# A fused attention and MoE kernel: one scale of s per chunk of tiles, the low parts of x on VectorE in every pair, the small products first in a tile, and the first loads on two queues

## The chip, the cores and the metric

The kernel runs on one core of a Trainium2 chip. The metric is the device time of one execution in microseconds (us): 1389.33 us, the median of 3 runs (1389.17 to 1389.57). Everything is float32 at the kernel's boundary except the two weight matrices, which come as float64.

## The reference

The input x has 8 batches of 4160 rows of 192 columns, which makes 33,280 tokens. A causal window of 7 taps is softmaxed for each of 8 heads and weighs the last 7 rows of x. The result goes through one MoE block with 1024 hidden columns.

```python
def _attn_ref(x, weight_gen):
    w = softmax(weight_gen, axis=-1)            # 8 heads, 7 taps
    ...
    out = np.einsum('bshk,bskhg->bshg', w, x_unf)
def _moe_ref(x, w_in, w_out, g_ln):
    h = x @ w_in
    h_max = np.max(h, axis=-1, keepdims=True)
    e = np.exp(h - h_max)
    sm = e / (np.sum(e, axis=-1, keepdims=True) + 1e-09)
    solu = h * sm
    mu = np.mean(solu, axis=-1, keepdims=True)
    var = np.mean((solu - mu) ** 2, axis=-1, keepdims=True)
    ln = (solu - mu) / np.sqrt(var + 1e-06) * g_ln
    return (ln @ w_out).astype(np.float32)
```

`w_in` and `w_out` arrive as the two 32-bit words of each double, and the kernel puts float32 numbers together from them on the chip.

## The kernel before, in words

**Tiling.** Each of the 128 partitions holds 260 consecutive tokens (`RUN`), so a batch of 4160 tokens lies on 16 partitions (`PB`), and a tile is one token of every partition: 128 rows. There are 260 tiles. The rows come in 18 chunks: one of 4 tiles, two of 8 and fifteen of 16. The attention works in groups of 4 tiles (the first group in two of 2), 66 groups in all, and TensorE turns the rows over two tiles at a time (a pair, 130 in all).

**The tokens before a run.** The window of a partition's first tokens reaches 6 tokens back (`HALO`), into the last tokens of the partition before it. L78 loads them for 127 partitions at once, with 1152 numbers each, into partitions 1 to 127. Where a batch begins the window holds zeros: L75 clears partition 0, and L80 copies a tile of zeros over the 8 partitions at which a batch begins. L79 loads the first four tiles themselves.

**A group of tiles.** The taps' softmax of a chunk is seven steps, t0 to t6: VectorE's maximum (L112), GpSimd's subtraction (L114), ScalarE's exponential (L118), VectorE's sum (L120), ScalarE's copy (L122), VectorE's reciprocal (L124) and GpSimd's product (L126). GpSimd then multiplies the seven shifted windows of x with the taps (L133), adds the products in two steps (L139, L141) and leaves two halves, `half`, which has two buffers. VectorE adds them into `a` (L366, the step `fin`, three buffers of four tiles) and ScalarE copies 64 of its columns once more (L372, `dup`).

**A pair.** TensorE transposes two tiles into `pa` (L383, `xT`), and ScalarE rounds them to a high part `x_hi` (L391, `xhi`). In every second pair TensorE then subtracts the high part in place (L398, `xn`) and ScalarE rounds the rest to `x_lo` (L405, `xlo`). In the pairs between, VectorE subtracts and rounds in one instruction (L412, `xld`). `VECTOR_PAIRS = 2` sets that.

**A tile.** The first product (`mm1`) fills one of three PSUM tiles `h` of 1024 columns: for each half of the columns three matmuls over 128 rows of x (L422), and then six over the 64 rows that are left, two of them on the two halves of the array's rows at a time (L427). VectorE takes the negated maximum of `h` (L441, `max`), bounds its size by the larger of it and 0.5 (L445, `vb`) and takes the reciprocal (L450, `vr`): that is the scale of s of that row. ScalarE makes the exponentials and their sum (L454, `exp`). VectorE multiplies h, scale and exponentials into s, over `h` itself, and sums it (L460, `solu`). ScalarE sums the squares (L466, `sq`) and rounds s to float16 (L473, `hi`). VectorE makes the float16 rest (L477, `lo`). SyncE's queue transposes both by DMA (L485, `tr`), and TensorE multiplies them with the prepared `w_out` in 24 matmuls (L529, `mm2`). ScalarE scales the result into `ot` (L540, `out`), and every four tiles are stored (L543, `od`). `mm1` of a tile waits until `sq` and `lo` of the tile three before it are done with `h`. The eight small steps f0 to f7 of a group of rows (`scales`: L497 on VectorE, L500 to L516 on ScalarE) make the last factor from the sums.

**The order.** Every engine runs its own list in order, and `issue_order` writes these lists: it walks through a model of the engines with a cost in ns for each step, and among the steps that are ready on an engine takes the one whose tile number plus the number in the table `URGENCY` is the smallest. Loads go to SyncE's queue in the order of the same walk; the weights' loads and the first two chunks' are issued ahead of it.

## Time and profile before

| | |
|---|---|
| median of 3 runs | 1389.33 us |
| the profiled execution | 1389.4 us |
| its span | 1387.5 us, so 1.9 us lie around it |
| TensorE clock granted | 0.991 |
| busy: TensorE matmul, VectorE, ScalarE, GpSimd | 1259.2, 1230.0, 1128.5, 1247.0 us |
| moved by DMA | 210.43 MB |

In a profile PE is TensorE, PEld its weight loads, DVE is VectorE, ACT ScalarE, POOL GpSimd and SP the SyncE queue. A row of the timeline gives the start, the duration, the engine, the line of the kernel and the operation, and in brackets how long the engine had been idle before it and what ended that. A row of the groups by line gives the busy time in all and the mean in ns. A row of the windows gives, for a stretch from one time to another, each engine's busy time and instructions. Busy shares of four engines between 81% and 91% of a span don't say by themselves which of them sets the end.

### The profile page before, as it was taken

How to read it: one execution, taken by the hardware profiler on the slowest of the kernel's cores; microseconds unless marked ns; L12 is line 12 of the kernel's file. 1: busy time of each engine (PE TensorE's matmuls, PEld its weight loads, DVE VectorE, ACT ScalarE, POOL GpSimd, SP SyncE). 2: the span in 40 equal slices, each digit the busy share in tenths (PEclk: the TensorE clock that was granted, in tenths of full speed). 3: DMA queues.
4: the chain of work that ended last, by engine and by line, in shares of the span. 5: the costliest groups of instructions: out<-in, count | busy, mean ns of one | idle time of the engine just before them, and what ended most of it. 6: DMA issues, size and time to landing. Idle time of an engine off the chain costs nothing.

```text
span 1387.5 us, 26562 instructions
## 1 busy us (share of the span) xinstructions
PE 1259.2 (91%) x10028; PEld 988.6 (71%) x10028; DVE 1230.0 (89%) x2068; ACT 1128.5 (81%) x2231; POOL 1247.0 (90%) x243
## 2 busy tenths in 40 slices
PE   0389899999999999989989999999999999999997
PEld 0267677777777777767767677777777777777776
DVE  2999898999989899889989898989899889999984
ACT  1588887888888888888888888888788888888885
POOL 1999999999999999999999999999999999999100
PEclk9989999999999999999999999999999999999999
DMA  3469768696968789697857768687858668766765
GB/s 90 139 142 194 147 128 201 124 207 122 194 130 174 146 145 195 122 198 123 186 130 166 158 149 186 118 190 145 193 109 191 146 140 176 132 133 117 134 131 116
DMA packets 565241, 210.43 MB, mean 152 GB/s; under 512 B 544329, under 2 KB 545785, under 8 KB 565112
## 3 DMA queue, kind: packets, MB, share of 16 engines
q1 hardware_dynamic: 565112, 208.73, 72.5%
q8 instruction: 79, 1.29, 0.4%
q14 instruction: 50, 0.41, 0.1%
HBM read 46.19 MB, written 25.56 MB: 52 GB/s over the span
## 4 chain that ended last, share of the span: by engine, by line
POOL 51%; DVE 16%; issue 13%; ACT 13%; PE 4%; DMA 3%; SPq 0%; POOLq 0%; DVEq 0%; ACTq 0%
POOL pr L133 27%; POOL pr L139 15%; POOL half L141 6%; DVE h L460 5%; ACT hl L473 4%; DVE hl L477 4%; ACT e L466 3%; DVE stats L441 3%; ACT e L454 3%; DVE a L366 3%; DMA xt<-in_x_dram 2%; POOL wt L114 2%; PE po L529 2%; POOL wt L126 1%; PE h L422 1%
## 5 line engine op out<-in xcount | busy, mean ns | idle before, releaser
L133 POOL TENSOR_TENSOR pr<-xt,wt 128x5376 f32<-128x5376 f32 (+1 forms) x66 | 631.3, 9565 | 23.1 <-DMA xt<-zeros 20.5
L529 PE MATMUL po<-w_hl,hlT 128*128 128x192 f16 x6192 | 558.5, 247 | 26.6 <-ACT ot L540 26.2
L529 PEld LDWEIGHTS <-hlT 128*128 128x128 f16 x6240 | 515.2, 98 | 82.2 <-issue 79.2
L477 DVE SCALAR_TENSOR_TENSOR hl<-h,hl 128x1024 f16<-128x1024 f32 x260 | 315.4, 1220 | 44.2 <-ACT e L466 31.5
L460 DVE SCALAR_TENSOR_TENSOR h<-h,stats,e 128x1024 f32<-128x1024 f32 x260 | 334.7, 1288 | 22.4 <-ACT e L454 9.2
L473 ACT ACTIVATE hl<-h 128x1024 f16<-128x1024 f32 x260 | 267.3, 1028 | 92.3 <-DVE stats L497 57.4
L139 POOL TENSOR_TENSOR pr<-pr 128x2304 f32<-128x2304 f32 (+1 forms) x66 | 332.7, 5041 | 5.2
L441 DVE TENSOR_REDUCE stats<-h 128x1 f32<-128x1024 f32 x260 | 316.1, 1216 | 8.9 <-PE h L427 8.1
L454 ACT ACTIVATE e<-h,stats 128x1024 f32<-128x1024 f32 x260 | 292.6, 1126 | 31.1 <-DVE stats L441 27.2
L466 ACT ACTIVATE e<-h,stats 128x1024 f32<-128x1024 f32 x260 | 292.3, 1125 | 5.9 <-DVE hl L477 5.4
L422 PE MATMUL h<-wa_hi,x_hi 128*128 128x512 f32 x520 | 225.4, 433 | 36.3 <-ACT e L466 22.8
L141 POOL TENSOR_TENSOR half<-pr 128x1536 f32<-128x1536 f32 (+1 forms) x66 | 225.8, 3422 | 5.2
L422 PE MATMUL h<-wa_hi,x_lo 128*128 128x512 f32 x520 | 207.5, 399 | 0.8 <-ACT x_lo L405 0.8
L422 PE MATMUL h<-wa_lo,x_hi 128*128 128x512 f32 x520 | 206.3, 397 | 0.0
L422 PEld LDWEIGHTS h<-wa_hi,x_hi 128*128 128x128 f32 x520 | 98.9, 190 | 59.3 <-ACT e L466 26.0
L427 PE MATMUL h<-wb_hi,x_hi 64*128 64x512 f32 x520 | 131.1, 500 | 0.0
L383 PE MATMUL pa<-ident,a 128*128 128x128 f32 x520 | 84.6, 286 | 44.2 <-DVE a L366 44.1
L540 ACT ACTIVATE ot<-po,stats 128x192 f32<-128x192 f32 x258 | 111.4, 432 | 8.5 <-PE po L529 8.5
L366 DVE TENSOR_REDUCE a<-half 128x768 f32<-128x1536 f32 (+1 forms) x66 | 116.4, 1764 | 1.6 <-POOL half L141 1.6
L427 PEld LDWEIGHTS h<-wb_hi,x_hi 64*128 64x128 f32 x520 | 48.6, 184 | 96.7 <-issue 96.7
L422 PEld LDWEIGHTS h<-wa_hi,x_lo 128*128 128x128 f32 x520 | 98.6, 190 | 24.3 <-ACT x_lo L405 1.6
L383 PEld LDWEIGHTS pa<-ident,a 128*128 128x128 f32 x520 | 55.8, 142 | 79.7 <-DVE a L366 44.1
(79 smaller groups left out, 1194.1 us busy)
## 6 DMA issues: line engine op xcount, KB each, us to landing
out_dram<-ot SPq DMA_DIRECT2D x65, 384.0 KB, 3.3
xt<-in_x_dram SPq DMA_DIRECT2D x30, 576.0 KB, 4.7
xt<-in_x_dram SPq DMA_DIRECT2D x30, 480.0 KB, 4.7
wt<-in_weight_gen_dram SPq DMA_DIRECT2D x15, 448.0 KB, 4.1
hlT<-hl SPq DMA_TRANSPOSE x260, 4.5
raw<-in_moe_w_out_dram SPq DMA_DIRECT2D x1, 1536.0 KB, 9.4
xt<-in_x_dram SPq DMA_DIRECT2D x3, 384.0 KB, 6.0
raw_a<-in_moe_w_in_dram SPq DMA_DIRECT2D x2, 512.0 KB, 11.5
```

The source lines that it names most:

```text
L133: nc.gpsimd.tensor_tensor(out=window(pr, 0, [(TG * D, K), (HG, n * H), (1, HG)]), in0=window(xt, t * D, [(D, K), (HG, n * H), (1, HG)]), i ...
L139: nc.gpsimd.tensor_tensor(out=pr[:, :3], in0=pr[:, :3], in1=pr[:, 3:6], op=ALU.add)
L141: nc.gpsimd.tensor_tensor(out=half, in0=window(pr, 0, [(2 * TG * D, 2), (D, n), (1, D)]), in1=window(pr, TG * D, [(5 * TG * D, 2), (D, n), ...
L422: nc.tensor.matmul(h[:, fs], lhs[:, 0, :], rhs[:, fs], start=n == 0, stop=False)
L427: nc.tensor.matmul(h[:, fs], lhs[rows, 1, :], rhs[rows], start=False, stop=n == 2,)
L441: nc.vector.tensor_reduce(stat(t, NMAX), h_of[t], axis=AX.X, op=ALU.max, negate=True)
L454: nc.scalar.activation(e, h_of[t], AF.Exp, bias=stat(t, NMAX), accum_out=stat(t, Z))
L460: nc.vector.scalar_tensor_tensor(out=h, in0=h, scalar=stat(t, SIGMA), in1=e, op0=ALU.mult, op1=ALU.mult, accum_out=stat(t, M))
L466: nc.scalar.activation(e_of.pop(t), h_of[t], AF.Square, bias=stat(t, M), scale=-float(FF), accum_out=stat(t, Q),)
L473: nc.scalar.activation(hl[:, 0, :], h_of[t], AF.Copy, scale=2.0**14)
L477: nc.vector.scalar_tensor_tensor(out=hl[:, 1, :], in0=h_of[t], scalar=2.0**14, in1=hl[:, 0, :], op0=ALU.mult, op1=ALU.subtract,)
L529: nc.tensor.matmul(po[:, :D], hlT[:, half * NJ + j, :], w2_hl[:, j, w, :], start=n == 0, stop=n == len(terms) - 1,)
```

## The change

Four things are changed, and the order of the work is made anew with them.

1. **The first loads.** L75 now clears the 6 tokens ahead on all 128 partitions, the loads of the tokens before a run are eight, one per batch, of 15 partitions each, and no zeros are copied. Half of the eight go to ScalarE's queue, and so do the first 128 rows of `w_in`, half of `w_out` and `g_ln`.
2. **The scale of s.** It is one number per partition and chunk, 1/(0.5 + norm), where the norm is the root of the sum of x's squares over this chunk and the one before it, times a factor from the largest sizes in `w_in`. The steps v00 to v03 square x on ScalarE, a quarter of a chunk at a time (L145, 768 numbers a partition), and v1 to v5 are seven instructions on one number a partition. n0 to n6 make the factor from `w_in` once. `vb` and `vr` are gone, and of f0 to f7 one activation and one reduction of a group are gone as well.
3. **x's low parts.** `VECTOR_PAIRS = 1`: every pair goes the way of L412, which is L479 now; `xn` and `xlo` no longer run.
4. **The order of a tile's matmuls.** The six over 64 rows (L491 now) come first in `mm1`, then the six over 128 rows (L494).

The table `URGENCY` and the model's costs are new (GpSimd's product and first sum of a group count 14990 ns instead of 14206, for example), and w_in's first 128 rows are converted ahead of its last 64.

```diff
-            nc.gpsimd.memset(xt[:1, : HALO * D], 0.0)
-            zeros = const.tile([B, D], F32, name="zeros")
-            nc.gpsimd.memset(zeros, 0.0)
-            nc.sync.dma_start(xv[1:, :HALO, :], x_run[: P - 1, RUN - HALO :, :])
+            nc.gpsimd.memset(xt[:, : HALO * D], 0.0)
             nc.sync.dma_start(xv[:, HALO : HALO + n, :], x_run[:, :n, :])
-            nc.sync.dma_start(
-                xv[::PB, :HALO, :], zeros.unsqueeze(1).broadcast_to([B, HALO, D])
-            )
+            for b in range(B):
+                queue = nc.sync if b % 2 else nc.scalar
+                queue.dma_start(
+                    xv[b * PB + 1 : (b + 1) * PB, :HALO, :],
+                    x_run[b * PB : (b + 1) * PB - 1, RUN - HALO :, :],
+                )
...
+            nc.scalar.activation(
+                junk[:, : (r1 - r0) * D].rearrange("p (t d) -> p t d", d=D), xv[:, r0:r1, :],
+                AF.Square, accum_out=squares_x[:, c + 1, part : part + 1],
+            )
...
     for f in range(2):
+        nc.scalar.dma_start(raw_a[:, f * FF : (f + 1) * FF], w_in[:P, f * FF : (f + 1) * FF])
         nc.sync.dma_start(raw_b[f * D2 : (f + 1) * D2, :], w_in[P:, f * FF : (f + 1) * FF])
...
-        for fs in halves:
-            for n, (lhs, rhs) in enumerate(((hi, wa_hi), (hi, wa_lo), (lo, wa_hi))):
-                nc.tensor.matmul(h[:, fs], lhs[:, 0, :], rhs[:, fs], start=n == 0, stop=False)
         for n, (lhs, rhs) in enumerate(((hi, wb_hi), (hi, wb_lo), (lo, wb_hi))):
             for f, fs in enumerate(halves):
                 rows = slice(f * D2, (f + 1) * D2)
-                nc.tensor.matmul(
-                    h[:, fs], lhs[rows, 1, :], rhs[rows], start=False, stop=n == 2,
-                )
+                nc.tensor.matmul(h[:, fs], lhs[rows, 1, :], rhs[rows], start=n == 0, stop=False)
+        for fs in halves:
+            for n, (lhs, rhs) in enumerate(((hi, wa_hi), (hi, wa_lo), (lo, wa_hi))):
+                nc.tensor.matmul(h[:, fs], lhs[:, 0, :], rhs[:, fs], start=False, stop=n == 2)
...
-            out=h, in0=h, scalar=stat(t, SIGMA), in1=e, op0=ALU.mult, op1=ALU.mult, accum_out=stat(t, M)
+            out=h, in0=h, scalar=row(t, SCALE), in1=e, op0=ALU.mult, op1=ALU.mult, accum_out=stat(t, M)
...
-VECTOR_PAIRS = 2
+VECTOR_PAIRS = 1
```

SyncE's queue at the start of the program, before: the taps of chunk 0 (`wt`), the last rows of `w_in` (`hl`), the tokens ahead of the runs (127 partitions), the first four tiles of x, and the first rows of `w_in` (`raw_a`) with the copy of zeros between their two halves.

```order
1 L96 DMA wt<-in_weight_gen_dram 128x224
2 L152 DMA hl<-in_moe_w_in_dram 64x1024 x2
3 L78 DMA xt<-in_x_dram 127x1152
4 L79 DMA xt<-in_x_dram 128x768
5 L168 DMA raw_a<-in_moe_w_in_dram 128x1024
6 L80 DMA xt<-zeros 8x6x192
7 L168 DMA raw_a<-in_moe_w_in_dram 128x1024
```

The same queue in the changed kernel, where `raw_101` is half of `w_out`:

```order
1 L96 DMA wt<-in_weight_gen_dram 128x224
2 L76 DMA xt<-in_x_dram 128x768
3 L79 DMA xt<-in_x_dram 15x1152 x4
4 L196 DMA hl<-in_moe_w_in_dram 64x1024 x2
5 L96 DMA wt<-in_weight_gen_dram 128x448
6 L202 DMA raw_101<-in_moe_w_out_dram 128x4x384
7 L85 DMA xt<-in_x_dram 128x1536
```

And ScalarE's list there, which issues its own loads ahead of its first arithmetic:

```order
1 L56 ACT_TABLE_LOAD
2 L79 DMA xt<-in_x_dram 15x1152 x4
3 L195 DMA raw_a<-in_moe_w_in_dram 128x1024 x2
4 L202 DMA raw_101<-in_moe_w_out_dram 128x4x384
5 L206 DMA g<-in_moe_g_ln_dram 128x8x1
6 L118 ACTIVATE wt<-wt 128x224
7 L145 ACTIVATE junk,squares_x<-xt 128x1920
8 L122 ACTIVATE wy<-wm 128x32
```

The 127 partitions have become eight times 15 on two queues, and the last rows of `w_in` have moved behind x.

TensorE near the program's start, before, where a pair's high part is subtracted (`minus`) and a tile's first product follows:

```order
93 L398 MATMUL pa<-x_hi,minus 128x256 x2
94 L422 MATMUL h<-wa_hi,x_hi 128x512
95 L422 MATMUL h<-wa_lo,x_hi 128x512
96 L422 MATMUL h<-wa_hi,x_lo 128x512
97 L422 MATMUL h<-wa_hi,x_hi 128x512
98 L422 MATMUL h<-wa_lo,x_hi 128x512
99 L422 MATMUL h<-wa_hi,x_lo 128x512
100 L427 MATMUL h<-wb_hi,x_hi 128x512 x2
101 L427 MATMUL h<-wb_lo,x_hi 128x512 x2
102 L427 MATMUL h<-wb_hi,x_lo 128x512 x2
```

And in the changed kernel:

```order
86 L491 MATMUL h<-wb_hi,x_hi 128x512 x2
87 L491 MATMUL h<-wb_lo,x_hi 128x512 x2
88 L491 MATMUL h<-wb_hi,x_lo 128x512 x2
89 L494 MATMUL h<-wa_hi,x_hi 128x512
90 L494 MATMUL h<-wa_lo,x_hi 128x512
91 L494 MATMUL h<-wa_hi,x_lo 128x512
92 L494 MATMUL h<-wa_hi,x_hi 128x512
93 L494 MATMUL h<-wa_lo,x_hi 128x512
94 L494 MATMUL h<-wa_hi,x_lo 128x512
```

The two subtractions of a pair are gone, and the paired small matmuls stand ahead.

VectorE in the middle of the program, before, up to a group's sum (`a`), with the two small instructions between a tile's maximum and its s:

```order
716 L445 TENSOR_REDUCE stats<-stats 128x1
717 L450 RECIPROCAL stats<-stats 128x1
718 L460 SCALAR_TENSOR_TENSOR h,stats<-h,stats,e 128x1024
719 L441 TENSOR_REDUCE stats<-h 128x1
720 L445 TENSOR_REDUCE stats<-stats 128x1
721 L450 RECIPROCAL stats<-stats 128x1
722 L477 SCALAR_TENSOR_TENSOR hl<-h,hl 128x1024
723 L366 TENSOR_REDUCE a<-half 128x4x192
```

And in the changed kernel, also up to a group's sum, where `wy` is the reciprocal of a chunk's taps (t5):

```order
706 L479 TENSOR_TENSOR x_lo<-pa,x_hi 128x512
707 L124 RECIPROCAL wy<-wy 128x128
708 L552 TENSOR_REDUCE stats<-stats 128x4
709 L532 SCALAR_TENSOR_TENSOR hl<-h,hl 128x1024
710 L515 SCALAR_TENSOR_TENSOR h,stats<-h,row,e 128x1024
711 L552 TENSOR_REDUCE stats<-stats 128x4
712 L505 TENSOR_REDUCE stats<-h 128x1
713 L433 TENSOR_REDUCE a<-half 128x4x192
```

Besides what is gone, the groups' sums have moved. In the list before, the sum of the group that begins at tile 32 stands behind 29 of the 260 instructions of L460, the one of tile 128 behind 121, and the last one, of tile 256, behind 244. In the changed list these are 29, 125 and 252. GpSimd's list holds the same 234 instructions in both from its first product on; only the taps' steps of the first few chunks of 16 tiles stand a group earlier or later.

More of the change, by code (lines that the diff above doesn't have):

```diff
@@ L232, in last_rows, with norm_of_first @@
             )
+    def norm_of_first(step):
+        if step < 3:
+            nc.vector.tensor_reduce(
+                sq[:, 4 + step : 5 + step], first["b" if step == 2 else step], axis=AX.X,
+                op=ALU.max, apply_absolute_value=True,
+            )
+        elif step == 3:
+            nc.scalar.activation(sq[:, 4:7], sq[:, 4:7], AF.Square)
+        elif step == 4:
+            first["total"] = ps_o.tile([P, 512], F32, name="po")
+            nc.tensor.matmul(first["total"][:, :3], ones, sq[:, 4:7], start=True, stop=True)
+        elif step == 5:
+            nc.vector.tensor_reduce(
+                first["total"][:, 8:9], first["total"][:, :3], axis=AX.X, op=ALU.add
+            )
+        elif step == 6:
+            nc.scalar.activation(column, first["total"][:, 8:9], AF.Ln, scale=1.05 * FF)
+            nc.scalar.activation(column, column, AF.Exp, scale=0.5)
     def first_rows(f, step):
@@ L278, in scale_and_sum @@
         elif step == 2:
-            junk = big.tile([P, FF], F32, name="e")
+            junk = big.tile([P, FH], F32, name="frac")
             nc.scalar.activation(
@@ L294, in prepare_second @@
         elif step == 5:
-            second["total"] = ps_a.tile([P, 512], F32, name="pa")
-            nc.tensor.matmul(second["total"][:, :NP], ones, sq, start=True, stop=True)
+            second["total"] = second["sums"][:, 256:]
+            nc.tensor.matmul(second["total"][:, :NP], ones, sq[:, :NP], start=True, stop=True)
         elif step == 6:
@@ L575, in tile_kernel @@
         ops[f"lx{n}"] = at_chunk(load_x, n)
-    for n in range(8):
+    for n in range(6):
         ops[f"f{n}"] = at(scales, n)
+    for n in range(7):
+        ops[f"n{n}"] = once(norm_of_first, n)
+    for n in range(1, 6):
+        ops[f"v{n}"] = at_chunk(norm_x, n)
+    for part in range(4):
+        ops[f"v0{part}"] = at_chunk(norm_x, 0, part)
     for n in range(TAP_STEPS):
@@ L635, in issue_order @@
             once(part + "4", DVE, 60 + 1.04 * size, part + "3")
+            once("n" + {"a0": "0", "a1": "1", "b": "2"}[part], DVE, 60 + 1.04 * size, part + "2")
         else:
@@ L645, in issue_order @@
     once("p4", ACT, 660, "p6")
+    once("n3", ACT, 100, "n0", "n1", "n2")
+    once("n4", PE, 220, "n3")
+    once("n5", DVE, 70, "n4")
+    once("n6", ACT, 400, "n5")
     for half in "01":
@@ L664, in issue_order @@
             add("lw", t, SP, 1270, last_group(c - 3))
-            add("lx0", t, SP, 1540, last_group(c - 2))
+            add("lx0", t, SP, 1540, last_group(c - 2), *parts_of(c - 2))
             for n in range(1, loads):
                 add(f"lx{n}", t, SP, 1540, (f"lx{n - 1}", t))
+        whole = starts[c + 1] - t == 16
+        for part in range(4 if whole else 1):
+            size = 830 if whole else 1800
+            if c > 1:
+                load = min(part + 1, loads - 1) if whole else loads - 1
+                add(f"v0{part}", t, ACT, size, (f"lx{load}", t))
+            else:
+                add(f"v0{part}", t, ACT, size, ready=15000)
+        add_norms(c, t)
         n = (starts[c + 1] - t) * 8
```

174 lines of the change are left out of this document (103 added, 71 removed).

## The prediction

> **What bounds the kernel now.** I read the busy times first, then GpSimd's timeline, then a window in the middle, the waits, and the two ends.
>
> ```profile
> span 1387.5 us, 26562 instructions
> PE 1259.2 (91%) x10028; PEld 988.6 (71%) x10028; DVE 1230.0 (89%) x2068; ACT 1128.5 (81%) x2231; POOL 1247.0 (90%) x243
> POOL 51%; DVE 16%; issue 13%; ACT 13%; PE 4%; DMA 3%; SPq 0%; POOLq 0%; DVEq 0%; ACTq 0%
> ```
>
> Three engines lie within 2% of each other, so the shares decide nothing. The chain of work that ended last lies on GpSimd (POOL) for half of the span. Its timeline has two idle places only, both at the start.
>
> ```profile
> 10.55 0.57 POOL L126 TENSOR_TENSOR wt<-wt,wy 128x224 f32<-128x224 f32 x1 [6.73 <-DVE wy L124]
> 31.59 4.95 POOL L133 TENSOR_TENSOR pr<-xt,wt 128x2688 f32<-128x2688 f32 x1 [20.46 <-DMA xt<-zeros]
> ...
> 1232.98 9.71 POOL L133 TENSOR_TENSOR pr<-xt,wt 128x5376 f32<-128x5376 f32 x1
> 1251.49 9.71 POOL L133 TENSOR_TENSOR pr<-xt,wt 128x5376 f32<-128x5376 f32 x1
> 1284.98 3.48 POOL L141 TENSOR_TENSOR half<-pr 128x1536 f32<-128x1536 f32 x1
> ```
>
> GpSimd begins at 31.59, ends at 1288.46 and never pauses between: 1256.9 us for 260 tiles, 4.83 a tile. But the program ends 99 us later. So the engines behind it (the downstream) lose ground on the way, and their own pace is the second thing to read: L460 makes two rows a tile.
>
> ```profile
> 250.00:1250.00 1000.00, 954.12 (x7658) 749.51 (x7656) 915.81 (x1528) 847.20 (x1666) 989.57 (x180) 1.00 0.76 157
> ...
> 250.00:1250.00 1000.00, 267.74 (x398) 1.00 0.76 157
> ```
>
> The columns are PE, PEld, DVE, ACT, POOL; the second row is L460 alone. That is 199 tiles in 1000 us, 5.025 a tile, with TensorE busy 95% of it. Why not 100%? The waits name one cause that is no shortage of an engine:
>
> ```profile
> ACT wt L118 <- POOL wt L114: 39.6, 15, 4.5
> ```
>
> In ScalarE's list the exponential of the taps stands earlier than GpSimd gets to the step ahead of it, so ScalarE, and all that waits for it, stands still 15 times. Near the end no taps are left, and there two tiles with a VectorE pair show what TensorE's own work allows:
>
> ```profile
> 1285.04 0.39 PE L422 MATMUL h<-wa_hi,x_hi 128*128 128x512 f32 x1
> 1294.24 0.48 PE L422 MATMUL h<-wa_hi,x_hi 128*128 128x512 f32 x1
> 1303.94 0.51 PE L398 MATMUL pa<-x_hi,minus 128*128 128x256 f32 x2 [0.20 <-ACT x_hi L391]
> 1304.29 0.39 PE L422 MATMUL h<-wa_hi,x_hi 128*128 128x512 f32 x1
> ```
>
> From 1285.04 to 1294.24 two tiles took 9.20, or 4.60 each, less than GpSimd's 4.83. The next two, whose pair has the subtraction L398 in it, took 10.05. So the kernel has two limits close together: GpSimd's unbroken list with its late start, and a downstream that could go faster than GpSimd but doesn't.
>
> **The start.** GpSimd's 20 us of idle time end with the zeros, which wait for the load of the tokens ahead of the runs:
>
> ```profile
> 2.46 26.27 DMA xt<-in_x_dram
> ...
> 31.08 0.69 DVE L194 TENSOR_SCALAR h<-raw_a 128x512 int32<-128x512 int32 x1 [20.61 <-DMA raw_a<-in_moe_w_in_dram]
> 31.81 0.69 DVE L197 TENSOR_SCALAR h<-raw_a 128x512 int32<-128x512 int32 x1
> GB/s 0 142 281 21 28 25 28 25 28 261 178 196 28 25 28 25 28 25 26 26 137 224 272 351 383 305 360 395 221 8 0 17 226 389 342 244 6 0 0 5
> ```
>
> The last row is the rate in slices of 1.5 us from 0 to 60. While that load ran alone the rate was 25 to 28 GB/s, against 395 at its best, and the load took 26 us. VectorE's conversions of `w_in` waited as long, 20.6 us, because half of `raw_a` was issued only after the zeros. The Trainium skill (DMA: Bandwidth & Descriptors, Why a DMA increments its semaphore by 16 and not by 1) says that the engines of a transfer are the largest number up to 16 that divides its first dimension, so 127 partitions run on one; this trace agrees, with a fifteenth of the best rate. By the same rule 15 partitions run on 15; no row here shows that.
>
> In the changed kernel I count what must land ahead of VectorE's first conversion: taps 112 KB, tokens 384 and 540 KB, the first half of `raw_a` 512 KB and, on the other queue meanwhile, 512 KB of `w_in`'s last rows; 2.1 MB at 395 GB/s is 5.3 us. For loads of 15 partitions there is no row; the nearest are those of 128, at up to 395 GB/s, and the one of 127 at 26. I take the first, since the eight hold only a quarter of the bytes, and keep the second as a rival. With the first issues at some 2 us, behind L75, and 2.0 for the landing of a small load,
>
> ```profile
> wt<-in_weight_gen_dram SPq DMA_DIRECT2D x1, 112.0 KB, 2.0
> 9.44 0.39 DVE L120 TENSOR_REDUCE wm<-wt 128x32 f32<-128x224 f32 x1 [1.43 <-ACT wt L118]
> ```
>
> that is 9.5. The taps' sum (L120) stands behind five conversions of 0.73 from start to start (the two rows at 31.08): 13.1. Sum 0.4, another conversion 0.7, reciprocal 0.4 and GpSimd's L126 0.6 give GpSimd's first product at 15.2 instead of 31.59. Bounds: 13, if the loads land at 7.5, and 20, if ScalarE, whose exponential now stands behind eight issues of its own, starts it only at 13. VectorE carries 3 reductions more there (n0 to n2, 0.7 each) and one conversion that used to be done while it waited, 4 us in all, so the downstream starts 16 to 17 us earlier, too.
>
> **The steady part.** Prices:
>
> ```profile
> L398 PE MATMUL pa<-x_hi,minus 128*128 128x256 f32 x130 | 32.5, 332 | 10.7 <-ACT x_hi L391 10.4
> L405 ACT CAST x_lo<-pa 128x512 fp32r<-128x512 f32 x65 | 38.9, 598 | 1.5 <-PE pa L398 1.4
> L412 DVE TENSOR_TENSOR x_lo<-pa,x_hi 128x512 fp32r<-128x512 f32 x65 | 44.3, 682 | 2.0 <-ACT x_hi L391 1.7
> L445 DVE TENSOR_REDUCE stats<-stats 128x1 f32<-128x2 f32 x260 | 38.2, 147 | 1.4
> L450 DVE RECIPROCAL stats<-stats 128x1 f32<-128x1 f32 x260 | 41.4, 159 | 5.1
> L318 ACT ACTIVATE w_hl<-h,k 128x768 f16<-128x768 f32 x2 | 1.8, 892 | 0.0
> L454 ACT ACTIVATE e<-h,stats 128x1024 f32<-128x1024 f32 x260 | 292.6, 1126 | 31.1 <-DVE stats L441 27.2 <-DVE stats L497 1.3 <-DVE stats L450 1.0
> L500 ACT ACTIVATE stats<-stats 128x4 f32<-128x4 f32 x63 | 15.2, 241 | 0.4
> ```
>
> TensorE loses L398's 32.5 us and the 10.7 that it waited there. VectorE loses L445 and L450, 79.6 us, and a reduction per group (67 at 0.15, 10), and gains 65 more low parts at 0.682, 44, and some 40 small instructions, 8: 37 less. ScalarE loses 65 roundings, 38.9, and 67 small activations at 0.24, 16. It gains 60 squares of 768 numbers between 0.89 (L318, the same width without a sum) and 1.13 (L454, wider and with a sum), 61 with 1.0, three wider ones, 5, and 18 chunks with five small ones, 22: 33 more, 1161 in all. GpSimd's list stays.
>
> The paired small matmuls come first in a tile. Their price today:
>
> ```profile
> 706.15 0.40 PE L422 MATMUL h<-wa_hi,x_lo 128*128 128x512 f32 x1
> 706.48 0.50 PE L427 MATMUL h<-wb_hi,x_hi 64*128 64x512 f32 x2
> 706.82 0.39 PE L427 MATMUL h<-wb_lo,x_hi 64*128 64x512 f32 x2
> 707.05 0.40 PE L427 MATMUL h<-wb_hi,x_lo 64*128 64x512 f32 x2
> 707.38 2.15 PE L529 MATMUL po<-w_hl,hlT 128*128 128x192 f16 x24
> ```
>
> A step without a change of form takes 0.23, the one into the small form 0.33 and then 0.34, the one out of it 0.33. A tile has one of each before and after, so I take 0; the ends are 0.1 a tile either way, 26 us of TensorE. All of that lies beside GpSimd as long as TensorE stays under 4.83.
>
> So each tile now needs 4.60 of TensorE, VectorE (1230 − 37)/260 = 4.59, ScalarE 4.47, and GpSimd 4.83. The changed list sets the sums of the groups accordingly: before, the last one stood behind 244 tiles' L460, now behind 252, so the downstream is meant to stay 3 to 4 tiles behind GpSimd all along. I forecast that GpSimd becomes the bound from its first product to its last.
>
> The tail then: the last sum (1.8), the copy (0.4) and the transposes (0.7), 2.9 us, and behind them in TensorE's list 6 first and 12 second products. Before, the last 12 second products (288 matmuls) and 5 first ones (30 of L422) filled the last 47.5 us, the final store among them, with TensorE busy for 39.4 of it:
>
> ```profile
> 1340.00:1387.50 47.50, 39.39 (x358) 33.52 (x358) 26.99 (x48) 29.01 (x58) 0.00 (x0) 0.96 0.63 123
> 1340.00:1387.50 47.50, 8.14 (x30) 5.28 (x30) 0.96 0.63 123
> 1340.00:1387.50 47.50, 26.55 (x288) 24.94 (x288) 0.96 0.63 123
> ```
>
> (All, L422, L529.) One more first product, 2.4, gives 2.9 + 47.5 + 2.4 = 52.8 with those waits. Without them, but with the last 3.8 us of output and store, it is 2.9 + 39.4 + 2.4 + 3.8 = 48.5; I take 50. The sum: 15.2 + 1256.9 + 50 = 1322.1 of span, and the 1.9 us between this execution's span and its own 1389.4 (the median of the runs is 1389.33, the same) make 1324.0.
>
> **The rivals.** *The downstream keeps setting the end.* Its offset today is 1389.4 − 260 × 5.025 = 82.9. With a start 16 earlier and (32.5 + 10.7)/260 = 0.166 off the pace that is 66.9 + 260 × 4.859 = 1330. For it: engines with one list each wait on each other, and 5% of idle time may stay. Against it: the waits on L114 go with a list that follows GpSimd's pace.
>
> *The pace doesn't move at all*, because ScalarE, with 33 us more and 60 long squares between the roundings that TensorE waits for, eats TensorE's gain: 1389.4 − 16 = 1373. Against it: ScalarE has 19% idle.
>
> *The tokens ahead of the runs stay slow.* Eight transfers of 69 KB, if one engine carried each as it did the 127 partitions, would need 2.7 us apiece at 26 GB/s, 21 in a row, and GpSimd would begin at 31 again: 1324 + 16 = 1340. The Trainium skill speaks for this where it says that transfers issued from several engines run on the same 16 DMA engines, so that two queues save issue time only (DMA: Bandwidth & Descriptors, Issuing engines are not separate DMA queues); then only the split in rows can bring the gain, which is how I counted it.
>
> *Slower than before.* GpSimd must now wait for no one, with the lists so close. Its product of the taps (L126) comes one group, 18.5 us, after L114, and VectorE's reciprocal for it (L124) stands only just ahead of the next group's sum in the new list. If the squares and their small steps make ScalarE and VectorE late there, GpSimd stops once in each of 17 chunks. From (1389.4 − 1324)/17 = 3.8 us a stop this gives back all; at 4.5, the longest wait between the two in the other direction today, it is 1400. Against it: from a group's sum to L124 the new list has about three tiles of VectorE's work, 14 us at 4.59, where GpSimd spends 20 on L114 and the next group.
>
> **How the numbers follow.** GpSimd's pace 0.62, the downstream's pace 0.20, slow tokens 0.06, unmoved pace 0.05, slower 0.03, and 0.04 for under 1312 (a start at 13 and a tail of 45 still give 13 + 1256.9 + 45 + 1.9 = 1317, so this needs a faster GpSimd as well). The likeliest gives 1324. The low end takes GpSimd's case down to that 1317 and leaves 5 for shorter rows, 1312; the high end reaches past the downstream's and the slow tokens' cases with some waits in them, 1346. A measurement of this kernel can't tell a difference under 0.2% from none. Faster by more than that 0.95, within it 0.02 (the unmoved pace with the start's gain lost as well), slower 0.03.
>
> **What would show it.** In the profile after, GpSimd's first product begins near 15 and its last ends near 1272, with under 5 us of idle time between; the wait of ScalarE on L114 shrinks to a few us; L515 has two rows per 4.83 us in the middle; VectorE waits for GpSimd's halves ahead of L433; and some 50 us follow GpSimd's end. I am wrong if GpSimd stands idle in the middle, if the time behind its end is 70 us or more, or if its first product begins after 20.

## The result, and the profile after

The changed kernel takes 1346.37 us (median of 4 runs, 1346.12 to 1347.67), before 1389.25 beside it: a ratio of 0.9693, 95% interval [0.9676, 0.971], 42.9 us less. I had said 1324, with 1312 to 1346. The profiled execution's page:

```profile
span 1345.8 us, 25810 instructions
PE 1246.8 (93%) x9900; PEld 970.8 (72%) x9900; DVE 1210.2 (90%) x1588; ACT 1162.8 (86%) x2318; POOL 1247.7 (93%) x241
ACT 43%; DVE 35%; issue 11%; PE 7%; DMA 2%; POOL 1%; SPq 0%; ACTq 0%; POOLq 0%
```

The chain that ended last has left GpSimd (51% before, 1% now) and lies on ScalarE and VectorE. GpSimd's timeline, its idle places and its two ends:

```profile
17.73 4.95 POOL L174 TENSOR_TENSOR pr<-xt,wt 128x2688 f32<-128x2688 f32 x1
...
38.12 0.97 POOL L126 TENSOR_TENSOR wt<-wt,wy 128x448 f32<-128x448 f32 x1 [0.42 <-DVE wy L124]
...
81.17 1.75 POOL L114 TENSOR_TENSOR wt<-wt,wm 128x896 f32<-128x896 f32 x1 [3.37 <-DVE wm L112]
...
102.13 1.76 POOL L126 TENSOR_TENSOR wt<-wt,wy 128x896 f32<-128x896 f32 x1 [0.78 <-ACT ot L591]
...
150.48 1.76 POOL L114 TENSOR_TENSOR wt<-wt,wm 128x896 f32<-128x896 f32 x1 [6.33 <-DVE row L151]
...
1286.95 3.48 POOL L182 TENSOR_TENSOR half<-pr 128x1536 f32<-128x1536 f32 x1
```

It starts 14 us earlier than before, waits 10.9 in all between its first product and 152, then hardly at all (nine waits of up to 0.5 on L552, 3.9 together), and ends at 1290.4, where I had 1272. The program ends 55 later. That looks like a bound; the experiments say that it isn't the only one.

The middle, all engines (PE, PEld, DVE, ACT, POOL) and L515 alone:

```profile
250.00:1250.00 1000.00, 976.32 (x7814) 761.00 (x7812) 924.31 (x1188) 894.66 (x1774) 985.66 (x178) 1.00 0.80 160
...
250.00:1250.00 1000.00, 275.41 (x410) 1.00 0.80 160
```

That is 205 tiles in 1000 us. Such a count is good to one tile only, 0.024 us a tile or some 6 us over 260; from the first of these rows of L515 to the last a tile takes 4.857 us (5.027 before, where the count gave 5.025). And the start of the downstream: VectorE's first conversion, and the first matmul of the first and of the ninth tile's first product, after and (second fence) before.

```profile
12.38 0.69 DVE L241 TENSOR_SCALAR h<-raw_a 128x512 int32<-128x512 int32 x1 [9.09 <-DMA raw_a<-in_moe_w_in_dram]
...
45.84 0.79 PE L491 MATMUL h<-wb_hi,x_hi 64*128 64x512 f32 x2
...
95.92 0.50 PE L491 MATMUL h<-wb_hi,x_hi 64*128 64x512 f32 x2
```

```profile
55.57 0.88 PE L422 MATMUL h<-wa_hi,x_hi 128*128 128x512 f32 x1
...
101.90 0.47 PE L422 MATMUL h<-wa_hi,x_hi 128*128 128x512 f32 x1 [0.39 <-DVE hl L477]
```

VectorE got its data 18.7 earlier, but the first product begins only 9.7 earlier, and the ninth tile's (the last row of each) only 6.0. How much of this lead lasts can be read from the rows that make s, one a tile: those of tiles 0, 30 and 259 (the first is 0), before and (second fence) after.

```profile
64.72 1.28 DVE L460 SCALAR_TENSOR_TENSOR h<-h,stats,e 128x1024 f32<-128x1024 f32 x1
...
218.39 1.29 DVE L460 SCALAR_TENSOR_TENSOR h<-h,stats,e 128x1024 f32<-128x1024 f32 x1
...
1368.74 1.28 DVE L460 SCALAR_TENSOR_TENSOR h<-h,stats,e 128x1024 f32<-128x1024 f32 x1
```

```profile
53.07 1.29 DVE L515 SCALAR_TENSOR_TENSOR h<-h,row,e 128x1024 f32<-128x1024 f32 x1 [1.27 <-ACT e L509]
...
218.41 1.28 DVE L515 SCALAR_TENSOR_TENSOR h<-h,row,e 128x1024 f32<-128x1024 f32 x1
...
1329.08 1.28 DVE L515 SCALAR_TENSOR_TENSOR h<-h,row,e 128x1024 f32<-128x1024 f32 x1
```

At tile 0 the changed kernel is 11.7 us ahead, at tile 30 not at all (1.6 at tile 20, 2.8 at tile 40). Its first 30 tiles took 165.3 us, where before took 153.7. From tile 30 to tile 259 a tile takes 4.850 us where it took 5.023, which makes 39.7 of the 41.7 us between the two spans; the other 2.0 lie behind the last of these rows. So nothing of the earlier start arrives at the end, and but for these 2 us the gain is the pace.

### The profile page after: what moved, and what is told of

It reads as the page before. It is cut to its first block, busy times and chain, and to the rows that moved or that the text cites. A ratio compares the mean times of both kernels' runs of the same rounds, so it can differ in the third digit from the quotient of the medians.

```text
span 1345.8 us, 25810 instructions
## 1 busy us (share of the span) xinstructions
PE 1246.8 (93%) x9900; PEld 970.8 (72%) x9900; DVE 1210.2 (90%) x1588; ACT 1162.8 (86%) x2318; POOL 1247.7 (93%) x241
## 4 chain that ended last, share of the span: by engine, by line
ACT 43%; DVE 35%; issue 11%; PE 7%; DMA 2%; POOL 1%; SPq 0%; ACTq 0%; POOLq 0%
ACT hl L528 12%; ACT e L521 12%; DVE h L515 11%; DVE hl L532 11%; ACT e L509 9%; DVE stats L505 5%; DVE a L433 4%; ACT junk L145 3%; PE po L580 3%; PE h L494 2%; ACT x_hi L458 2%; ACT ot L591 2%; DMA hlT<-hl 2%; PE h L491 1%; DVE x_lo L479 1%
## 5 line engine op out<-in xcount | busy, mean ns | idle before, releaser
L580 PEld LDWEIGHTS <-hlT 128*128 128x128 f16 x6240 | 505.9, 98 | 83.2 <-issue 75.5
L515 DVE SCALAR_TENSOR_TENSOR h<-h,row,e 128x1024 f32<-128x1024 f32 x260 | 333.8, 1285 | 19.1 <-ACT e L509 16.9
L528 ACT ACTIVATE hl<-h 128x1024 f16<-128x1024 f32 x260 | 266.0, 1029 | 98.4 <-DVE h L515 55.4
L532 DVE SCALAR_TENSOR_TENSOR hl<-h,hl 128x1024 f16<-128x1024 f32 x260 | 316.5, 1218 | 36.8 <-ACT e L521 34.4
L180 POOL TENSOR_TENSOR pr<-pr 128x2304 f32<-128x2304 f32 (+1 forms) x66 | 333.0, 5045 | 5.2
L521 ACT ACTIVATE e<-h,stats 128x1024 f32<-128x1024 f32 x260 | 293.0, 1127 | 1.1 <-DVE hl L532 1.0
L494 PE MATMUL h<-wa_hi,x_hi 128*128 128x512 f32 x520 | 234.0, 450 | 0.0
L494 PE MATMUL h<-wa_lo,x_hi 128*128 128x512 f32 x520 | 206.4, 397 | 0.0
L494 PE MATMUL h<-wa_hi,x_lo 128*128 128x512 f32 x520 | 205.9, 396 | 0.0
L494 PEld LDWEIGHTS h<-wa_hi,x_hi 128*128 128x128 f32 x520 | 98.1, 189 | 107.1 <-issue 95.5
L491 PE MATMUL h<-wb_hi,x_hi 64*128 64x512 f32 x520 | 131.0, 499 | 17.1 <-DVE hl L532 11.2
L494 PEld LDWEIGHTS h<-wa_hi,x_lo 128*128 128x128 f32 x520 | 98.4, 189 | 23.2
L494 PEld LDWEIGHTS h<-wa_lo,x_hi 128*128 128x128 f32 x520 | 99.0, 190 | 12.0
L491 PE MATMUL h<-wb_hi,x_lo 64*128 64x512 f32 x520 | 104.2, 395 | 0.0
L450 PE MATMUL pa<-ident,a 128*128 128x128 f32 x520 | 81.2, 278 | 23.9 <-DVE x_lo L479 13.2
```

The costliest lines, as they stand in the source:

```text
L180: nc.gpsimd.tensor_tensor(out=pr[:, :3], in0=pr[:, :3], in1=pr[:, 3:6], op=ALU.add)
L491: nc.tensor.matmul(h[:, fs], lhs[rows, 1, :], rhs[rows], start=n == 0, stop=False)
L494: nc.tensor.matmul(h[:, fs], lhs[:, 0, :], rhs[:, fs], start=False, stop=n == 2)
L515: nc.vector.scalar_tensor_tensor(out=h, in0=h, scalar=row(t, SCALE), in1=e, op0=ALU.mult, op1=ALU.mult, accum_out=stat(t, M))
L521: nc.scalar.activation(e_of.pop(t), h_of[t], AF.Square, bias=stat(t, M), scale=-float(FF), accum_out=stat(t, Q),)
L528: nc.scalar.activation(hl[:, 0, :], h_of[t], AF.Copy, scale=2.0**14)
```

## The experiments

Sixteen kernels ran. All ratios are to the kernel before, run beside them. A pace below is the time from tile 30's s to tile 259's, divided by 229.

**The matmul order.** In the changed kernel, before's order:

```diff
+        for fs in halves:
+            for n, (lhs, rhs) in enumerate(((hi, wa_hi), (hi, wa_lo), (lo, wa_hi))):
+                nc.tensor.matmul(h[:, fs], lhs[:, 0, :], rhs[:, fs], start=n == 0, stop=False)
         for n, (lhs, rhs) in enumerate(((hi, wb_hi), (hi, wb_lo), (lo, wb_hi))):
...
-        for fs in halves:
-            for n, (lhs, rhs) in enumerate(((hi, wa_hi), (hi, wa_lo), (lo, wa_hi))):
-                nc.tensor.matmul(h[:, fs], lhs[:, 0, :], rhs[:, fs], start=False, stop=n == 2)
```

> The changed kernel with the matmul order of before in a tile (128-row products first, then the 64-row pairs); everything else as changed. Theory A (GpSimd alone sets the end; the new order costs TensorE 0.1 us a tile, 4.48 instead of about 4.38 for its two products, but beside GpSimd): GpSimd's end stays at 1290 +- 2, only the tail shortens by the 6 first products left in it, so 1346 becomes 1343 to 1346, and TensorE's busy time falls by some 20 to 26 from 1246.8. Rival B (TensorE sets the pace): 260 x 0.1 = 26 less, 1320 to 1326. Rival C (the order costs nothing, my price in the prediction): TensorE's busy time within 5 of 1246.8 and the time within 1 of 1346.

Measured 1347.24 us, 0.9694 [0.9681, 0.9707]: no difference. The edit the other way round, the new order in the kernel before:

> The kernel before with nothing changed but the matmul order in a tile (64-row pairs first). If the order costs TensorE 0.1 us a tile, 20 to 26 of busy time more (1259 becomes 1280 to 1285), and since TensorE was busy for 95.4% of the steady part there, nearly all of it shows: 1405 to 1415. If the order costs nothing (my price): 1389 +- 2. If the pairs in front let TensorE begin a tile earlier (it needs only half of its buffer's width first): below 1387.

Measured 1390.09, 1.0002 [0.9993, 1.001]. The order does cost TensorE something. The group of the first 128-row matmul (busy time, mean in ns, idle time before) in the changed kernel, and the busy times with the same group in e1:

```profile
L494 PE MATMUL h<-wa_hi,x_hi 128*128 128x512 f32 x520 | 234.0, 450 | 0.0
```

```profile
PE 1231.8 (91%) x9900; PEld 967.9 (72%) x9900; DVE 1209.2 (90%) x1588; ACT 1161.7 (86%) x2318; POOL 1247.6 (93%) x241
L490 PE MATMUL h<-wa_hi,x_hi 128*128 128x512 f32 x520 | 228.4, 439 | 19.5 <-DVE hl L535 13.1 <-ACT e L524 6.4
```

15 us of TensorE's time come free in e1 and turn into waiting. The pace is 4.850 in the changed kernel and 4.851 in e1. So TensorE, busy for 97.6% of the middle, doesn't set the pace. The theory that I had formed on the trace after, TensorE 0.1 a tile slower and with it the kernel, fell here.

**The early squares.** L145 reads a constant in place of x, and so waits for no load.

```diff
-                junk[:, : (r1 - r0) * D].rearrange("p (t d) -> p t d", d=D), xv[:, r0:r1, :],
+                junk[:, : (r1 - r0) * D].rearrange("p (t d) -> p t d", d=P),
+                ident.unsqueeze(1).broadcast_to([P, (r1 - r0) * D // P, P]),
```

> The changed kernel whose squares (L145) read a constant matrix instead of x, at the same place in ScalarE's list and at the same width, so that no square waits for a load of x; the scale of s is then another number, which leaves every duration as it is. Theory A (the squares' waits at 130 and 139 us hold up ScalarE, through it VectorE's maximum for the next taps, and so GpSimd's L114 by 6.33): GpSimd's waits before 152 fall from 10.9 to under 4.5, and the end comes 6 to 9 earlier, 1337 to 1340. Rival B (the downstream is at its own limit behind GpSimd): GpSimd ends 6 to 9 earlier but the tail grows by as much, 1344 to 1346. Rival C (the stall comes from the slow TensorE clock at 63 to 88 and the transposes in SyncE's queue, not from the squares): GpSimd's waits stay, 1346.

Measured 1343.90, 0.9669 [0.9656, 0.9682], 2.5 less at the medians (the two intervals overlap). GpSimd's wait on L151 fell to 2.4, but others took its place (4.1 on L112, 2.5 on L126), and it ended at 1289.2 instead of 1290.4. Theory A of it holds for a small part only.

**GpSimd out of the way.** Without L180:

```diff
-        nc.gpsimd.tensor_tensor(out=pr[:, :3], in0=pr[:, :3], in1=pr[:, 3:6], op=ALU.add)
```

> The changed kernel without L180 (the sum over three of the seven taps is left out): GpSimd needs 5.1 less a group, 4.82 - 1.28 = 3.54 a tile. The time that is left is the downstream's own. Theory A (the downstream, ScalarE and VectorE and TensorE waiting on each other, stands at a limit of its own close to GpSimd's): 4.7 to 4.8 a tile, 1315 to 1335. Rival B (GpSimd alone was the bound, TensorE has 4.60 to 4.70 a tile and runs through): TensorE begins at about 45 and is busy for 1247, so 1295 to 1310.

Measured 1345.71, 0.9682 [0.9667, 0.9697]. A quarter of GpSimd's work is gone and nothing is gained. GpSimd's groups of the taps now:

```profile
L114 POOL TENSOR_TENSOR wt<-wt,wm 128x896 f32<-128x896 f32 (+2 forms) x18 | 29.0, 1613 | 106.2 <-DVE wm L112 94.3 <-DVE row L151 11.9
L126 POOL TENSOR_TENSOR wt<-wt,wy 128x896 f32<-128x896 f32 (+2 forms) x18 | 29.0, 1613 | 205.9 <-DVE stats L551 179.5 <-DVE wy L124 18.8 <-ACT ot L590 7.7
```

It waits for VectorE, chunk after chunk. Tiles 30 and 259 in this run:

```profile
215.96 1.28 DVE L514 SCALAR_TENSOR_TENSOR h<-h,row,e 128x1024 f32<-128x1024 f32 x1
...
1326.60 1.28 DVE L514 SCALAR_TENSOR_TENSOR h<-h,row,e 128x1024 f32<-128x1024 f32 x1
```

That is 4.850 a tile, the changed kernel's pace to a thousandth. So the downstream has a limit of its own at 1345, and it isn't GpSimd (my forecast) that makes it; the expectation's rival B fell, and theory A's 1315 to 1335 was too low.

**A like cut on each of the other engines**, on top of e4, to see which of them is that limit:

```diff
-                junk[:, : (r1 - r0) * D].rearrange("p (t d) -> p t d", d=D), xv[:, r0:r1, :],
+                junk[:, :D], xv[:, r0, :],
```

> The kernel of the run without L180 (1345.7 us, GpSimd out of the way), and each square L145 takes 192 numbers of x instead of 768 (the scale of s is too small a number for that, durations stay): ScalarE is lighter by 60 x 0.4 to 0.5, 25 to 32 us, all of it where the squares stand. Theory A (in the part of each chunk where squares, row steps and taps meet, ScalarE is full, 9.9 of 10 us, and VectorE and TensorE wait for it): most of it shows, 1316 to 1328. Rival B (VectorE is the bound) and rival C (TensorE is): at most 5 less, 1340 or more. Rival D (three fixed lists wait for each other everywhere alike): about a third of it, 8 to 11 less, 1335 to 1338.

```diff
-        nc.vector.tensor_reduce(stat(t, NMAX), h_of[t], axis=AX.X, op=ALU.max, negate=True)
+        nc.vector.tensor_reduce(stat(t, NMAX), h_of[t][:, :880], axis=AX.X, op=ALU.max, negate=True)
```

> The kernel without L180, and the maximum L505 goes over 880 of the 1024 columns of h (the last 144 are left out of it): 0.15 to 0.17 less a tile, 39 to 44 us off VectorE, evenly along the run. Theory A (ScalarE full where the squares are, VectorE only elsewhere): half or less, 10 to 20, 1326 to 1336. Rival B (VectorE is the bound): 35 to 44 less, 1302 to 1311. Rival C (TensorE is): at most 5 less. Rival D: 10 to 15 less.

```diff
-        terms = [(half, j, w) for j in range(NJ) for half, w in ((0, 0), (0, 1), (1, 0))]
+        terms = [(half, j, w) for j in range(NJ) for half, w in ((0, 0), (0, 1), (1, 0))][:-2]
```

> The kernel without L180, and the second product leaves out its last two matmuls of 24: 2 x 0.086 = 0.17 a tile, 45 us off TensorE, evenly. Rival C (TensorE is the bound): 35 to 45 less, 1301 to 1311. Theory A: only in the parts where ScalarE isn't full, at most 10 to 15 less, 1330 or more. Rival B: at most 5 less. Rival D: 10 to 15 less.

| | cut | time, us | ratio and interval | gain over e4 |
|---|---|---|---|---|
| e5 | ScalarE 27.6 us | 1329.71 | 0.9575 [0.9559, 0.9591] | 16.0 |
| e6 | VectorE 36.9 us | 1338.30 | 0.9635 [0.962, 0.9649] | 7.4 |
| e7 | TensorE 38.5 us | 1344.95 | 0.9682 [0.9668, 0.9697] | 0.8 |

(The cuts are the differences of the pages' busy times to e4's.) A us of these squares is worth 0.58, one of the maximum on VectorE 0.2, one of the second product on TensorE nothing that can be measured. The cut on ScalarE is bunched where the squares stand and the other two are even, so the three differ by place as well as by engine. Some 5 us of e5's 16 come before tile 30 (210.81 in it, 215.96 in e4); behind it the pace falls from 4.850 to 4.804, in e6 to 4.817, and e7 has 4.855. Of the three pieces cut, the squares that the change added are the dearest. Where they hurt is seen in the windows of the changed kernel, ten us each, in the columns PE, PEld, DVE, ACT, POOL:

```profile
680.00:690.00 10.00, 9.46 (x79) 7.29 (x77) 9.31 (x11) 8.88 (x19) 9.92 (x2) 1.00 1.07 248
690.00:700.00 10.00, 10.00 (x78) 7.79 (x77) 8.98 (x15) 9.94 (x23) 9.92 (x4) 1.00 0.99 216
700.00:710.00 10.00, 9.31 (x78) 7.17 (x77) 9.42 (x12) 9.97 (x21) 9.92 (x2) 1.00 0.58 109
710.00:720.00 10.00, 10.00 (x77) 7.78 (x77) 10.00 (x15) 8.66 (x21) 9.40 (x4) 1.00 0.69 144
...
730.00:740.00 10.00, 10.00 (x79) 7.60 (x78) 8.90 (x13) 7.91 (x16) 9.84 (x3) 1.00 0.71 149
```

From 690 to 710 ScalarE is full: three of a chunk's four squares, most of the row's steps and the taps' exponential stand there. From 710 on it waits for VectorE again. Within one chunk the limit passes from one engine to another, and what one had spare can't be used while the other is full. The groups show both sides of it, 98 us of ScalarE's idle time and 80 of VectorE's:

```profile
L528 ACT ACTIVATE hl<-h 128x1024 f16<-128x1024 f32 x260 | 266.0, 1029 | 98.4 <-DVE h L515 55.4 <-DVE stats L552 42.3 <-DVE row L162 0.4
L532 DVE SCALAR_TENSOR_TENSOR hl<-h,hl 128x1024 f16<-128x1024 f32 x260 | 316.5, 1218 | 36.8 <-ACT e L521 34.4 <-ACT hl L528 0.7
L552 DVE TENSOR_REDUCE stats<-stats 128x4 f32<-128x8 f32 (+3 forms) x201 | 31.4, 156 | 43.1 <-ACT e L521 40.3 <-ACT stats L567 1.1 <-ACT stats L561 0.2
```

VectorE's L532 waits for ScalarE's L521 though it needs nothing that L521 writes; both read `h`. The Trainium skill (PSUM — Partial Sum Buffer, PSUM bank collisions raise a hardware error) says that two engines may not touch one bank of PSUM at a time, reads against reads included, and that the compiler's scheduler puts a dependency between such instructions. This trace agrees, with 34.4 us of waiting.

**The loads.** In the changed kernel, the first loads of before:

```diff
-            nc.gpsimd.memset(xt[:, : HALO * D], 0.0)
...
-                    xv[b * PB + 1 : (b + 1) * PB, :HALO, :],
-                    x_run[b * PB : (b + 1) * PB - 1, RUN - HALO :, :],
+            nc.sync.dma_start(xv[1:, :HALO, :], x_run[: P - 1, RUN - HALO :, :])
...
```

> The changed kernel with the first loads of before (127 rows of tokens in one transfer, the zeros behind them, all on SyncE's queue, in before's order). GpSimd's first product goes back from 17.7 to about 31. Theory A (the downstream sets the end, and its first product hung on VectorE's conversions, 45.8 against 55.6 before): the first product of TensorE at 52 to 56 again, and the end 5 to 10 later, 1351 to 1356. My prediction's view (GpSimd sets the end from its first product on): 14 later, 1360. Rival (the start is absorbed before tile 40): within 2 of 1346.

Measured 1365.13, 0.9829 [0.9815, 0.9844], 18.8 more, which is more than each theory had. VectorE's first conversion and TensorE's first product in it:

```profile
31.44 0.69 DVE L238 TENSOR_SCALAR h<-raw_a 128x512 int32<-128x512 int32 x1 [26.07 <-DMA raw_a<-in_moe_w_in_dram]
...
63.78 0.79 PE L488 MATMUL h<-wb_hi,x_hi 64*128 64x512 f32 x2
```

The conversions begin 19.1 later, the first product 17.9, the end 18.8: the shift goes through one to one, and in size it goes with `raw_a` rather than with GpSimd's first product (14.2 later). The row also shows what the change's other parts cost at the start: with the same loads before's first product began at 55.57, now it is 63.78, 8.2 later.

The other way round, the kernel before with the new loads alone:

> The kernel before with the first loads of the changed one and nothing else changed. If the start's gain holds to the end (as 18.8 was lost when the changed kernel got the old loads): 1370 to 1376, the first product of TensorE at 38 to 42 instead of 55.6. If before's list makes GpSimd wait for other things early: 1376 to 1385.

Measured 1374.38, 0.9895 [0.988, 0.991], 15.0 less, and the first product begins at

```profile
40.67 0.88 PE L422 MATMUL h<-wa_hi,x_hi 128*128 128x512 f32 x1
```

14.9 earlier. Again one to one; GpSimd's first product moved by nearly as much here, 14.6, so this run doesn't tell the two apart. Tiles 0 and 30:

```profile
50.15 1.28 DVE L460 SCALAR_TENSOR_TENSOR h<-h,stats,e 128x1024 f32<-128x1024 f32 x1
...
203.85 1.29 DVE L460 SCALAR_TENSOR_TENSOR h<-h,stats,e 128x1024 f32<-128x1024 f32 x1
```

Its lead on the kernel before is 14.6 at the first and 14.5 at the second: the loads alone keep what they gain. The changed kernel has the same loads, and at tile 30 it is 14.6 behind this one, 2.9 of that at tile 0 already. So the rest of the change costs about as much at the start as the loads bring. What takes it is only known in part: the squares have a share, since the first 30 tiles shrink from 165.3 to 163.8 in e3 and to 160.6 in e11 below, but nothing that ran gives the 153.7 of before.

**The squares in the whole kernel.** As e5, with L180 in its place:

> The changed kernel with GpSimd whole, its squares over 192 instead of 768 numbers (29 us less on ScalarE; with GpSimd's L180 left out the same cut took 1345.7 to 1329.7). If GpSimd is no wall here either: 1330. If GpSimd, which ended at 1290 and waited for nothing from 152 us on, stands right behind the downstream: its end moves only by the early waits, to 1284 to 1289, and with 50 us behind it the whole is 1335 to 1340.

Measured 1337.54, 0.9622 [0.9609, 0.9635]; GpSimd ends at

```profile
1281.72 3.49 POOL L182 TENSOR_TENSOR half<-pr 128x1536 f32<-128x1536 f32 x1
```

1285.2, with 51 us of span behind it. Without L180 the same cut had given 1329.7. So GpSimd is a second limit, at 1337: some 8 us below the first.

**The squares spread over the chunk.** In `issue_order`, ahead of its return:

```diff
+    for c in range(4, len(starts) - 1):
+        s = starts[c]
+        for n, name in enumerate(("v00", "v01", "v03", "v02", "v1", "v2", "v3", "v4", "v5")):
+            ahead = (20, 16, 12, 8, 6, 5, 4, 3, 2)[n]
+            place = order.index(("exp", max(s - ahead, 0)))
+            if order.index((name, s)) < place:
+                order.remove((name, s))
+                order.insert(order.index(("exp", max(s - ahead, 0))) + 1, (name, s))
```

> The kernel without L180 (1345.7), with the four squares and five small row steps of each 16-tile chunk spread over it (one square behind the exponential of every fourth tile, then the small steps tile by tile) instead of bunched in some five tiles; same work. Theory A (ScalarE is full only where they are bunched, 9.9 of 10 us at 690 to 710, and has 1 to 2 us of 10 to spare elsewhere): the bunch's stall goes, and the pace falls from 4.88 towards TensorE's 4.76, by 10 to 25 us, 1320 to 1336. Rival D (the sum of the work on three lists counts, not its place): within 3 of 1345.7. Rival E (a square between other steps is in the way everywhere: it delays each fourth tile's roundings): slower, 1350 or more.

> The same spreading in the changed kernel with GpSimd whole; the early squares stand later than their loads there. Theory A with GpSimd right behind: GpSimd loses its early waits on L112 and L151 in part, and the end is 1332 to 1341. Rival D: 1344 to 1347. Rival E: 1350 or more.

Measured 1336.72, 0.9615 [0.9602, 0.9628] without L180, and 1339.18, 0.9636 [0.9622, 0.9649] with it. The work is the same, only its place differs, and it is worth 9.0 and 7.2 us. In e10 the pace falls from 4.850 to 4.822. Rivals D and E fall. ScalarE is still full in one stretch of e11, where the taps stand, and GpSimd ends 8.0 earlier:

```profile
680.00:690.00 10.00, 9.43 (x77) 7.19 (x74) 8.77 (x13) 9.70 (x23) 9.92 (x4) 1.00 0.92 187
690.00:700.00 10.00, 9.89 (x84) 7.82 (x82) 9.64 (x13) 9.88 (x19) 9.92 (x2) 1.00 0.61 128
700.00:710.00 10.00, 9.92 (x81) 7.61 (x79) 10.00 (x15) 8.84 (x21) 9.92 (x4) 1.00 0.76 134
...
1278.97 3.49 POOL L182 TENSOR_TENSOR half<-pr 128x1536 f32<-128x1536 f32 x1
```

With chunk 0's taps ahead of the conversions as well:

```diff
+    ctx.enter_context(tc.manual_schedule())
     for step in range(TAP_STEPS):
         softmax_taps(0, step)
```

> As the run before, and chunk 0's taps stand ahead of the conversions in VectorE's list, so that L126 no longer waits 13.3 us for L124: GpSimd's first product at 10 to 11 instead of 17.7. If GpSimd is the wall behind the spread squares, its end comes 4 to 7 earlier and the time falls by as much, 1327 to 1336. If the downstream is (its first product hung on the conversions, at 45.8), the time is within 2 of the run before.

Measured 1334.81, 0.9608 [0.9594, 0.9621], the best version. GpSimd's start, 6.6 earlier than in e11, is mostly lost again at once: it waits 4.2 at the next taps for L124, which stands among the conversions, and its end is 1.9 earlier.

```profile
10.91 4.95 POOL L174 TENSOR_TENSOR pr<-xt,wt 128x2688 f32<-128x2688 f32 x1
...
35.03 0.97 POOL L126 TENSOR_TENSOR wt<-wt,wy 128x448 f32<-128x448 f32 x1 [4.17 <-DVE wy L124]
...
1277.06 3.50 POOL L182 TENSOR_TENSOR half<-pr 128x1536 f32<-128x1536 f32 x1
```

A try at more, with two squares of 1536 numbers a chunk in place of four of 768, and before's matmul order:

```diff
-                r0 = r0 + part * TC // 4
-                r1 = r0 + TC // 4
+                if part % 2 == 0:
+                    return
+                r0 = r0 + (part - 1) * TC // 4
+                r1 = r0 + TC // 2
```

> Spread squares in two instructions of 1536 a chunk instead of four of 768 (0.8 us of ScalarE less a chunk, 12 in all), chunk 0's taps ahead of the conversions, matmul order of before. If ScalarE's list and GpSimd's end both still count: 3 to 8 less than 1334.8, 1327 to 1332. If GpSimd's end plus 52 sets the time alone: 1333 to 1335. If the 1.5 us squares are in ScalarE's way: 1336 or more.

Measured 1341.48, 0.966 [0.9646, 0.9675]: worse. TensorE waits 29.3 us for ScalarE's L597 (`out`), which was 5.9 in e12. That fits squares that are in the way, but two things were changed, and which of them did it stays open.

**What the pace's gain was made of.** The old way for every other pair, at the place of the new one:

```diff
+    def low_of_before(t):
+        if t // 2 % 2:
+            low_x_on_vector(t)
+        else:
+            subtract_high(t)
+            low_x(t)
```

> The changed kernel, but every other pair's low part is made as before (matmuls with minus on TensorE, rounding by ScalarE), at the same place in the order. ScalarE +39, TensorE +32, VectorE -44. Theory A (ScalarE's work counts most, by the cuts 0.55 us per us there and 0.19 on VectorE): +21 - 8, 1357 to 1363. Rival C (TensorE): +32, 1375 or more. Rival (the VectorE way costs as much as it saves): within 3 of 1346.

Measured 1413.37, 1.0177 [1.0162, 1.0192], 67 more, far over what the engines' sums give. TensorE isn't the reason, since it is busy for only 941 us of the middle's 1000. Two waits (us in total, times, longest) are new or larger:

```profile
PE pa L450 <- ACT x_lo L472: 48.7, 53, 4.2
DVE hl L539 <- ACT e L528: 96.1, 79, 4.2
```

Its transposes wait for ScalarE's rounding, which stands at a place that the order had chosen for VectorE. So e13 shows what a step costs at a place that wasn't planned for it, and not what this part of the change brought; that stays open.

The two small instructions a tile, put back:

```diff
+        nc.vector.tensor_reduce(
+            again[:, :1], stat(t, NMAX), axis=AX.X, op=ALU.max, apply_absolute_value=True
+        )
...
+        nc.vector.reciprocal(again[:, 1:], again[:, :1])
```

> The changed kernel with two small VectorE instructions a tile put back (a maximum over one number behind L505 and a reciprocal ahead of L515, on a tile that nobody else reads), 260 x (0.147 + 0.159) = 80 us of VectorE. By the slope of the cut on VectorE (7.4 of 39, 0.19): +15, 1358 to 1364. If VectorE is over the edge with 4.96 a tile: 1380 or more. If it has room: within 5 of 1346.

Measured 1368.01, 0.9854 [0.9837, 0.987], 21.6 more. The two rows add up to 80.2 us, but VectorE's busy time grew by 51.2 only (1210.2 to 1261.4), since small instructions overlap with their neighbours. By that it is 0.42 a us, twice what the cut of e6 gave. So the one scale a chunk takes two small instructions off every tile, which is worth about 22, and pays for that with squares of which three quarters of the width cost 16 (e5), or 9 (e9) while GpSimd stands behind.

## Why the prediction was wrong

The direction held, the size didn't: 1324 against 1346, just past the upper end of the range.

- **The step that failed** is "I forecast that GpSimd becomes the bound from its first product to its last". I compared sums per tile (4.60, 4.59, 4.47 against GpSimd's 4.83) and took the three smaller ones for free. They aren't: the three lists that wait for each other take 4.850 a tile, the same with a quarter of GpSimd's work gone (e4), although none of them has more than 4.74 of work in the middle (TensorE, 97.6% of 4.857). e5 to e7 show that of the pieces tried the squares on ScalarE count most, e10 that their bunching is part of it.
- **Along my own sum** the profiled execution is 23.7 over: GpSimd's first product 2.5 later, 15.8 more from there to its end (10.9 of waits before 152, 3.9 in the nine small ones, the rest slower rows), and 5.4 more behind it, 55.4 instead of 50. The 10.9 lie in the first 30 tiles, where the downstream loses its lead; my sum had no term for that.
- **Two of the sums per tile were off.** TensorE's 4.60 came from two tiles near the end; its busy time less L398's gives (1259.2 − 32.5)/260 = 4.72. VectorE became 19.8 us lighter, not 37: the 79.6 us of L445 and L450 were durations, and these overlap with their neighbours (e14).
- **ScalarE's 33 us more** were counted right (1128.5 became 1162.8) and priced at nothing, for its 19% of idle time. The 27.6 us of them that e5 took off were worth 16. An average of idle time is no cover for work that is bunched.
- **"The downstream starts 16 to 17 us earlier"**: its data did, 18.7, its first product 9.7, its tile 30 not at all. I priced the work added there at 4 us; up to the first product e8 puts it at 8.2 and e15, with the new loads, at 45.84 − 40.67 = 5.2. Part of it is no work of VectorE: ScalarE's exponential of the second taps stands ahead of the conversions' steps and waits for GpSimd's first group. From the first conversion to the first product it took 33.5 us, and 31.5 with that group shorter (e4). The larger loss, 11.7 us more in the first 30 tiles than before, I hadn't counted at all, and what makes it stays open but for the squares' share.
- **The rival that came true** is the downstream that keeps setting the end. I had 66.9 + 260 × 4.859 = 1330. Its pace was right (4.850 from tile 30 on, 4.857 between 250 and 1250); the 16 us that it lacked are about the 16 of the earlier start in its 66.9. It had a chance of 0.20. That the high end of the range, 1346, lies so near the measured time is luck, since no term of the sum led there.
- **GpSimd's own case was off, too.** With the downstream lightened (e9) the time is 1337.5, not 1324: the start 3.2 later (18.44 against 15.2), waits for VectorE early on, and 51 us behind its end instead of 50. In the changed kernel `raw_a` was issued at 6.1 and landed at 12.4, where I had some 2 and 9.5 (the parts named there, 2, 5.3 and 2.0, make 9.3). "GpSimd must now wait for no one" was the rival on the slower side; it stopped in the first few chunks, 10.9 us in all, and in the 17 chunks only nine times and for at most 0.5.
- **Right**: the matmul order at 0 (e1, e2), though for another reason than I gave, since it does cost TensorE 10 to 15 us that nobody waits for; the wait of L118 on L114 nearly gone (39.6 to 4.7); 15 partitions a load (67.5 KB landed in 4.0 us, where the one of 127 had taken 26), so the rival of the slow tokens fell.
- **The tests I named** as signs of being wrong didn't catch the error: GpSimd started before 20, didn't stand idle in the middle and had 55 us behind its end, under the 70. The signs of being right did: its end at 1290 instead of 1272, and 14.8 us of idle time instead of under 5. An unbroken list on one engine is what a tie looks like as well; only taking work off it (e4) tells.
